# Sigmoid attention and a SiLU feed-forward on one core: four sums of x handed out one burst later in three out stages

## The chip, the core and the metric

The kernel runs on one core of a Trainium2 chip. The metric is the device time of one execution in microseconds (us), the median of several runs. PE is the engine of matmuls (PEld its loads of weights), DVE the vector engine, ACT the scalar engine with its function tables, POOL GpSimd, which issues the loads here, and SP the engine that issues the stores and the transposing DMAs. A bank is one of eight buffers in which PE leaves its results and from which DVE and ACT read them.

## The reference

```python
# q, k, v: 8 batches x 12 heads x 448 rows x 64;  w_in: 768 x 2048;  w_out: 2048 x 768
scores = q @ k.T / sqrt(64) - log(448)
attn   = sigmoid(scores) @ v                       # no softmax: no sum over a row
x      = attn.transpose(0, 2, 1, 3).reshape(3584, 768)
h      = x @ w_in
out    = (h * sigmoid(h)) @ w_out                  # float32, 3584 x 768
```

## The kernel before, in words

**Attention.** A group is four heads of one batch, so there are 24 groups, three to a batch. Each has seven rounds. A round, `scores`, is four small matmuls for scores (L223) and one sigmoid over 128 x 896 on ACT (L230). When a group's seven rounds are over, `values` multiplies by v in 28 matmuls into two banks (L254), and two scalings on DVE (L265, 128 x 448 each) move the result into xT, the transposed x of that batch in 16 bits.

**Feed-forward.** From the second pair of batches on, both products are done by a scheme of seven products in place of eight on 2 x 2 blocks (Strassen's, in Winograd's form), two batches at a time. That needs sums of the operands. `x_sums` (L355) makes four of the halves of xT for the first product: three go to tiles tx, one overwrites a half of xT. It does so in two goes: for the first two thirds of the columns' groups (four instructions over 128 x 896) once the first five of the pair's six groups have their values, and for the last third (128 x 448) behind the last group's values. `h_pair` then runs the seven products by x and w_in (L376) and SiLU.

`out_set` does the second product for two blocks of 128 rows: seven products of eight matmuls each (L502, 128 x 384 columns), with sums of the operands S made by DVE ahead (L510, L511, L514, L518) and read out by DVE. The products and what empties their banks are, in order: 1: L513; 2: L517, with the operand sum L518 behind it; 3: L523; 4: L526; 5: L529; 6: L534 and L535; 7: L539. Stores (L495) go out on SP's queue. `out_set` is a generator which gives one matmul at a time: 56 steps to a set. What an instruction on DVE stands behind is decided only by the order in which the Python code issues them; each engine takes its own in that order.

**The out stages.** For m = 0, 1 and 2 the out sets of the batches 2m and 2m + 1 (three sets for m = 0 and 2, four for m = 1) run amid the attention of the next two batches. This stage lies at some 74 to 120 us, 154 to 209 us and 242 to 289 us. Of the eight banks, six are three double buffers for scores and values, and two are left for the out matmuls; so a product waits until the one two before it has been read out. The order is a list written out by hand of pairs (rounds of scores, out matmuls behind them), such as (2, 9) or (3, 16). For each pair `burst` issues its rounds of scores and, where a group is complete, that group's `values`; it returns whether there were values. Behind it and after half of its out matmuls, `rows_if_any` is called. Behind the values of the pair's fifth group, `after_values` puts a generator with the four sums on a list, and each call of `rows_if_any` issues one of them; it also issues, where there is any, a copy with a transposing DMA for a later group. Five calls issue the four sums and take the generator off. A last burst or two follow, then what is left of the out matmuls, and the stage behind (`h_pair`), which begins with two products, the last group's values and the last third of the sums.

For m = 0 and 2 the fifth group's values stand in burst 16 of 18 (two rounds, two out matmuls), followed by (2, 9) and (3, 13). For m = 1 they stand in burst 14 of 16 (two rounds, six out matmuls), followed by (3, 16) and (2, 10).

The last out stage (m = 3) has no attention beside it and no sums of x.

Of the kernel before, what the change touches and what calls it, by code (L numbers as in the profile page):

```python
# [17 lines left out]
def kernel(  # L18
# [9 lines left out]
    nc = tc.nc  # L28
# [35 lines left out]
    def banks_for_attention(doubles):  # L64
        psum.close()
        banks.clear()
        bufs_of.update(double=doubles, single=NBANK - 2 * doubles)
        for name, bufs in bufs_of.items():
            taken[name] = 0
            new_pool(name, bufs)  # L70
# [7 lines left out]
    def banks_for_h():  # L78
        doubles = [[2 * i, 2 * i + 1] for i in longest_idle("double")]
        ring[:] = sum(doubles[:-2], [])  # L80
        ring.extend(2 * bufs_of["double"] + i for i in longest_idle("single"))
        ring.extend(sum(doubles[-2:], []))
        psum.close()
        banks.clear()
        new_pool("any", 1)
        for i in range(NBANK):
            banks[i] = banks["any"].tile([P, 512], F32, tag=f"any{i}", name=f"any{i}")
# [117 lines left out]
    def dma_transpose(g, name, copy):  # L205
        if ("k", g) not in qkT:
            new_qkT(g)
        rows = p2.tile([P, NCH, 2, D], F16, tag=f"{name}r", name=f"{name}r")
        copy(rows, flat[name, g].rearrange("p j c d -> p c j d"))
        nc.sync.dma_start_transpose(  # L210
            out=qkT[name, g], in_=rows.rearrange("p c j d -> p (c j d)")
        )
# [3 lines left out]
    def scores(g, ch):  # L216
        attnT[g, ch] = p12.tile([P, 2, S], F16, tag="attnT", name="attnT")
        psc = two_banks("psc")
        for half in range(2):
            own = slice(half * HP, (half + 1) * HP)  # L220
            for j in range(2):
                rows = slice(j * D, (j + 1) * D)
                nc.tensor.matmul(  # L223
                    psc[own, j, :S],
                    qkT["k", g][rows, ch, own],
                    qkT["q", g][rows, :, own],
                    start=True,
                    stop=True,
                )
        nc.scalar.activation(attnT[g, ch], psc[:, :, :S], AF.Sigmoid, bias=bias_s, scale=QKSCALE)  # L230
# [7 lines left out]
    def values(g, end=NCH):  # L238
        b, iq = divmod(g, NQ)
        if b not in xT:  # L240
            assert b < 2 or b - 2 in h_done
            xT[b] = p2.tile([P, NPAIR, S], F16, tag="xT", name="xT")
        pav, done_rounds = part_of.pop(g, None) or (None, 0)
        if pav is None and bufs_of["double"] > 2 and "any" not in banks:
            both = two_banks("pav")
            pav = [both[:, half] for half in range(2)]
        elif pav is None:
            pav = [one_bank("pav") for _ in range(2)]
        for ch in range(done_rounds, end):
            at = attnT.pop((g, ch))  # L250
            for half in range(2):
                own = slice(half * HP, (half + 1) * HP)
                for j in range(2):
                    nc.tensor.matmul(  # L254
                        pav[half][j * D : (j + 1) * D, :S],
                        flat["v", g][own, j, ch, :],
                        at[own, j, :],
                        start=(ch == 0),
                        stop=(ch == NCH - 1),
                    )  # L260
        if end < NCH:
            part_of[g] = pav, end
            return
        for half in range(2):
            nc.vector.tensor_scalar_mul(xT[b][:, half * NQ + iq, :], pav[half][:, :S], SX)  # L265
        if iq == NQ - 1:
            ready.add(b)
# [196 lines left out]
    def w_sums():  # L464
        for i in (2, 3, 4):
            tw[i] = cpool.tile([P, NHC, NO2], F16, tag=f"T{i}", name=f"T{i}")
        tw[1] = wq[0][1]
        for o, x, y in (
            (tw[3], wq[1][1], wq[0][1]),
            (tw[1], wq[0][1], wq[0][0]),  # L470
            (tw[2], wq[1][1], tw[1]),
            (tw[4], tw[2], wq[1][0]),
        ):
            for f in range(0, NHC, 2):
                nc.vector.tensor_sub(o[:, f : f + 2], x[:, f : f + 2], y[:, f : f + 2])
                yield
# [71 lines left out]
    sums = w_sums()  # L548
# [21 lines left out]
    def sets(m):  # L570
        for g in range(0, NCH - 1, 2):
            step = out_set(
                block(m, g), row_blocks(m, g), block(m, g + 1), row_blocks(m, g + 1)
            )
            for i, ns in enumerate(step):
                if m == 0 and g == 0 and i in (10, 14):
                    next(sums)
                if m == 0 and g == 0 and i in (20, 28, 36, 44):
                    next(in_sums)
                yield ns  # L580
        if m % 2 == 1:
            g = NCH - 1
            yield from out_set(
                kept, row_blocks(m - 1, g), block(m, g), row_blocks(m, g), m == B // 2 - 1
            )

    later, sums_of_x = [], []

    def rows_if_any(before, copy):
        if sums_of_x and next(sums_of_x[0], "end") == "end":  # L590
            sums_of_x.pop()
        if later and later[0][0] < before:
            g, name = later.pop(0)
            dma_transpose(g, name, copy)
            if name == "q":
                behind_rows(g, before)
# [3 lines left out]
    def behind_rows(g, before):  # L600
        if g + 3 >= NQB:
            return
        if g + 3 < before:
            load("kq", g + 3)
            return
        held.append(g + 3)
        if g + 1 == before:
            nc.gpsimd.tensor_copy(gate, qkT["q", g][:1, 0, :1])
            for to in held:
                load("kq", to)  # L610
            held.clear()
# [54 lines left out]
    def values_if_any():  # L666
        if waiting:
            g = waiting.pop(0)
            values(g)
            after_values(g)  # L670
            return True
        return False
# [68 lines left out]
    def burst(n, size=2):  # L741

        new = units[n : n + size]
        for u in new:
            scores(*u)
        with_values = values_if_any()
        for g, ch in new:
            if ch == NCH - 1:
                waiting.append(g)
                if 9 <= g + 3 < NQB:  # L750
                    later.extend(((g + 3, "k"), (g + 3, "q")))
        return with_values
# [16 lines left out]
    for m in range(B // 2 - 1):  # L769
        banks_for_attention(3)  # L770
        nc.scalar.activation(warm, bias_s, AF.Sigmoid)
        stream = sets(m)
        for _ in range(FIRST_DENSE):
            next(stream)
        bursts = FOUR_SETS if m % 2 else THREE_SETS
        assert sum(size for size, _ in bursts) == 2 * NT_B
        own = 2 * NQ * (m + 2)
        n = 2 * NT_B * (m + 1)
        for size, count in bursts:
            burst(n, size)  # L780
            n += size
            rows_if_any(own, nc.vector.tensor_copy)
            for i in range(count):
                next(stream)
                if i == count // 2:
                    rows_if_any(own, nc.vector.tensor_copy)
        assert not sums_of_x
        nc.scalar.activation(warm, bias_s, AF.Silu)
        for _ in stream:
            pass  # L790
        (g,) = waiting
        waiting.clear()
        banks_for_h()

        def last_values():
            values(g)
            after_values(g)
            for _ in x_sums(m + 1, NQ - 1, NQ):
                pass
            nc.gpsimd.tensor_copy(gate, tx[m + 1, 4][:1, NQ - 1, :1])  # L800

        for i, _ in enumerate(h_pair(m + 1, last_values)):
            if i % 8 == 7:
                rows_if_any(NQB, nc.gpsimd.tensor_copy)
# [33 lines left out]
```

## Time and profile before

| what | value |
|---|---|
| median of 3 runs | 365.05 us (364.96 to 365.18) |
| the profiled execution, whole | 365.46 us |
| its span, first to last instruction | 363.5 us |
| granted clock of PE | 0.997 |
| busy: PE, DVE, ACT, POOL | 98%, 69%, 69%, 21% of the span |
| one of the 12 sums over 128 x 896 (L355) | 0.61 to 0.62 us |

The page's first part gives each engine's busy time and share of the span. Matmuls are pipelined: a row of several in turn gives the start of the first and the time to the modelled end of the last. The view of waits says which engine waited for whom, in total, how often, and the longest. In the order of time each row has a start in us from the span's start, a length, an engine, a line, the written and read tiles and how many instructions are merged; brackets give the idle time before it and what ended it. Where nothing is known to have ended it, it is put under "issue".

### The profile page before, as it was taken

Reading aid. Unit: us, or ns where it says so; the run is one execution under the profiler, and the core shown is the slowest. Engines: PE = TensorE matmul, PEld = TensorE weight load, DVE = VectorE, ACT = ScalarE, POOL = GpSimd, SP = SyncE. Lnnn points to the kernel's source line nnn. Section 1 sums busy time; section 2 is a strip of 40 time slices with the busy share of each in tenths; the row PEclk is TensorE's granted clock in tenths of the full one; section 3 lists DMA queues with packets and bytes.
Section 4 is the critical chain, followed back from the end, with each engine's and each line's share of the span. In section 5 each row is a group of like instructions: output and inputs, shape, how many; then the busy total and the mean of one; then the engine's idle time right before and its main releaser. Section 6 shows DMA issues by size and latency. Waiting matters only on the chain. (4 is left out here: it accounts for less than half of the span.)

```text
span 363.5 us, 7651 instructions
## 1 busy us (share of the span) xinstructions
PE 356.1 (98%) x3036; PEld 186.8 (51%) x3036; DVE 252.2 (69%) x459; ACT 249.3 (69%) x339; POOL 77.5 (21%) x116
## 2 busy tenths in 40 slices
PE   8999999999999999999999999999999999999995
PEld 6554445555555555555555455554555555556662
DVE  3565469787666587868566768795856677797763
ACT  5999886479989756688777746679899956640000
POOL 8666511040060272000033047000100000000000
PEclk9999999999999999999999999999999999999998
DMA  8999999979969599008679569802983120003333
GB/s 138 198 204 203 204 205 203 172 114 194 163 115 207 119 133 172 0 2 160 104 133 193 105 130 165 122 2 51 166 100 88 25 65 0 3 0 88 87 88 87
DMA packets 65859, 42.80 MB, mean 118 GB/s; under 512 B 36128, under 2 KB 62496, under 8 KB 65824
## 3 DMA queue, kind: packets, MB, share of 16 engines
q0 software_dynamic: 27072, 22.58, 42.6%
q1 hardware_dynamic: 38320, 19.34, 28.0%
q8 instruction: 24, 0.39, 0.5%
q10 hardware_dynamic: 432, 0.39, 0.3%
q14 instruction: 11, 0.09, 0.1%
HBM read 45.61 MB, written 11.01 MB: 156 GB/s over the span
## 5 line engine op out<-in xcount | busy, mean ns | idle before, releaser
L230 ACT ACTIVATE attnT<-psc,bias_s 128x896 f16<-128x896 f32 x168 | 157.9, 1009 | 20.6 <-PE psc L223 19.3
L502 PEld LDWEIGHTS <-S 128*128 128x128 f16 x448 | 42.0, 98 | 33.6 <-issue 8.1
L223 PE MATMUL psc<-qT,kT 64*64 64x448 f16 x672 | 48.9, 360 | 1.1 <-ACT attnT L230 0.8
L265 DVE TENSOR_SCALAR xT<-pav 128x448 f16<-128x448 f32 x48 | 27.7, 620 | 28.9 <-PE pav L254 28.9
L502 PEld LDWEIGHTS <-gTr 128*128 128x128 f16 x336 | 31.1, 98 | 27.3 <-issue 8.7
L124 POOL DMA_DIRECT2D vf<-in_v_dram x24 | 17.3, 723 | 129.7 <-PE pav L254 122.6
L502 PE MATMUL po<-w_out_sb,gTr 128*128 128x384 f16 x224 | 41.6, 327 | 0.0
L376 PEld LDWEIGHTS <-w_in_sb 128*128 128x128 f16 x288 | 27.9, 98 | 26.7 <-issue 1.1
L502 PE MATMUL po<-T,S 128*128 128x384 f16 x224 | 41.0, 327 | 0.0
L502 PE MATMUL po<-w_out_sb,S 128*128 128x384 f16 x224 | 40.8, 326 | 0.0
L286 PE MATMUL ph<-xT,w_in_sb 128*128 128x448 f16 x192 | 38.5, 353 | 0.0
L254 PE MATMUL pav<-attnT,vf 64*64 64x448 f16 x672 | 38.1, 351 | 0.1
L376 PE MATMUL pa<-xT,w_in_sb 128*128 128x448 f16 x144 | 33.2, 353 | 0.0
L223 PEld LDWEIGHTS <-kT 64*64 64x64 f16 x672 | 17.9, 104 | 27.8 <-issue 21.3
L376 PEld LDWEIGHTS <-SI 128*128 128x128 f16 x216 | 21.1, 98 | 20.0 <-issue 0.5
L254 PEld LDWEIGHTS <-vf 64*64 64x64 f16 x672 | 21.6, 106 | 12.3 <-issue 2.9
L286 PEld LDWEIGHTS <-w_in_sb 128*128 128x128 f16 x192 | 17.8, 98 | 18.9 <-issue 3.4
L392 ACT ACTIVATE part<-pa 128x448 f32<-128x448 f32 x24 | 12.7, 543 | 18.1 <-PE pa L376 18.1
L502 PE MATMUL po<-T,gTr 128*128 128x384 f16 x112 | 21.9, 327 | 0.6 <-DVE osb L523 0.6
L370 ACT ACTIVATE gTr<-pc 128x448 f16<-128x448 f32 x24 | 13.1, 544 | 12.9 <-DVE pc L386 12.5
L386 DVE TENSOR_TENSOR part<-pb,part 128x448 f32<-128x448 f32 x24 | 14.9, 622 | 8.3 <-ACT part L392 5.0
L184 ACT ACTIVATE m<-po 128x384 f32<-128x384 f32 x1 | 0.5, 491 | 27.3 <-PE po L502 27.3
(76 smaller groups left out, 471.1 us busy)
## 6 DMA issues: line engine op xcount, KB each, us to landing
out_dram<-osb SPq DMA_DIRECT2D x52, 192.0 KB, 3.2
vf<-in_v_dram POOLq DMA_DIRECT2D x24, 224.0 KB, 6.6
kf<-in_k_dram POOLq DMA_DIRECT2D x23, 224.0 KB, 7.4
qf<-in_q_dram POOLq DMA_DIRECT2D x23, 224.0 KB, 7.8
w_in_sb<-in_moe_w_in_dram POOLq DMA_DIRECT2D x16, 192.0 KB, 7.9
w_out_sb<-in_moe_w_out_dram POOLq DMA_DIRECT2D x4, 768.0 KB, 14.9
out_dram<-osb SPq DMA_DIRECT2D x6, 96.0 KB, 2.2
kT<-kr SPq DMA_TRANSPOSE x18, 5.1
```

The source lines that it names most:

```text
L124: nc.gpsimd.dma_start(flat[name, g][:, :, c0:c1].rearrange("p i c d -> p i (c d)"), rows_in(name, g)[:, :, c0 * D : c1 * D],)
L184: nc.scalar.activation(o, i, AF.Copy)
L223: nc.tensor.matmul(psc[own, j, :S], qkT["k", g][rows, ch, own], qkT["q", g][rows, :, own], start=True, stop=True,)
L230: nc.scalar.activation(attnT[g, ch], psc[:, :, :S], AF.Sigmoid, bias=bias_s, scale=QKSCALE)
L254: nc.tensor.matmul(pav[half][j * D : (j + 1) * D, :S], flat["v", g][own, j, ch, :], at[own, j, :], start=(ch == 0), stop=(ch == NCH - 1),)
L265: nc.vector.tensor_scalar_mul(xT[b][:, half * NQ + iq, :], pav[half][:, :S], SX)
L286: nc.tensor.matmul(ph[:, :S], w_in_sb[:, cc, fc * P : (fc + 1) * P], xT[b][:, cc, :], start=(at == 0), stop=(at == NCC - 1),)
L370: nc.scalar.activation(gTr[:, r * NG + i, col + c * S : col + (c + 1) * S], h, AF.Silu, bias=0.0, scale=ISX)
L376: nc.tensor.matmul(to, w[:, n, i * P : (i + 1) * P], x[:, n], start=(start and n == 0), skip_group_check=not start, stop=(n == NQ - 1),)
L386: nc.vector.tensor_add(o, po, x)
L392: nc.scalar.activation(got[i, 1], bank[i, "a"], AF.Copy)
L502: nc.tensor.matmul(po[:, :NO2], a[:, fc, :], w[:, fc, :], start=(fc == 0), stop=(fc == NHC - 1))
```

## The change

`rows_if_any` gets a flag. With the flag off it issues no sum of x; the copies with transposing DMAs are not touched. Behind a burst with values and amid its out matmuls the flag is off. So the four sums stand behind and amid the next two bursts, which are the last two of the stage, and the generator is taken off after the loop.

```diff
-    def rows_if_any(before, copy):
-        if sums_of_x and next(sums_of_x[0], "end") == "end":
-            sums_of_x.pop()
+    def rows_if_any(before, copy, sums=True):
+        if sums and sums_of_x:
+            next(sums_of_x[0])
         if later and later[0][0] < before:
             g, name = later.pop(0)
             dma_transpose(g, name, copy)
...
         for size, count in bursts:
-            burst(n, size)
+            with_values = burst(n, size)
             n += size
-            rows_if_any(own, nc.vector.tensor_copy)
+            rows_if_any(own, nc.vector.tensor_copy, not with_values)
             for i in range(count):
                 next(stream)
                 if i == count // 2:
-                    rows_if_any(own, nc.vector.tensor_copy)
-        assert not sums_of_x
+                    rows_if_any(own, nc.vector.tensor_copy, not with_values)
+        assert next(sums_of_x.pop(), "end") == "end"
```

The order on DVE at the three places, before and after:

```
m = 0, 2  before: L265 x2, sum 1, sum 2, sum 3, L526, sum 4, L529, L534
          after:  L265 x2, sum 1, L526, sum 2, sum 3, L529, sum 4, L534
m = 1     before: L265 x2, sum 1, L517, L518, sum 2, sum 3, L523, sum 4, L526, L529, L534
          after:  L265 x2, L517, L518, sum 1, L523, sum 2, L526, sum 3, L529, sum 4, L534
```

## The prediction

> **What bounds the kernel now.** I read the page's first part, then the waits of PE, and then the order of time around the sums of x in each of the three out stages that have them.
>
> ```profile
> PE 356.1 (98%) x3036; PEld 186.8 (51%) x3036; DVE 252.2 (69%) x459; ACT 249.3 (69%) x339; POOL 77.5 (21%) x116
> ```
>
> PE is the bound from end to end. Work that moves on DVE alone, as here, is worth only the time that PE stands still for it. The waits of PE (what it waited for, us in total, times, longest) name all that the profile sees as such:
>
> ```profile
> PE pw L181 <- DVE bias_s L624: 1.1, 1, 1.1
> PE psc L223 <- ACT attnT L230: 0.8, 2, 0.5
> PE po L502 <- DVE osb L523: 0.6, 1, 0.6
> ```
>
> One row belongs to the out matmuls: one wait of 0.6 us on DVE's L523. The order of time of the second of the three stages (m = 1) shows the place; columns are start, length, engine, line, and in brackets the idle time before it.
>
> ```profile
> 200.56 1.16 DVE L265 TENSOR_SCALAR xT<-pav 128x448 f16<-128x448 f32 x2 [1.17 <-PE pav L254]
> ...
> 201.63 0.61 DVE L355 TENSOR_TENSOR tx<-xT 128x896 f16<-128x896 f16 x1
> ...
> 202.16 0.55 DVE L517 TENSOR_TENSOR osb<-po,m 128x384 f32<-128x384 f32 x1
> ...
> 202.21 2.12 PE L502 MATMUL po<-T,S 128*128 128x384 f16 x12
> 202.63 0.68 DVE L518 TENSOR_TENSOR S<-gTr,S 128x1024 f16<-128x1024 f16 x1
> 203.23 0.62 DVE L355 TENSOR_TENSOR tx<-xT,tx 128x896 f16<-128x896 f16 x1
> 203.76 0.62 DVE L355 TENSOR_TENSOR xT<-xT 128x896 f16<-128x896 f16 x1
> ...
> 204.30 0.55 DVE L523 TENSOR_TENSOR osb<-po,m 128x384 f32<-128x384 f32 x1
> 204.77 0.62 DVE L355 TENSOR_TENSOR tx<-xT,tx 128x896 f16<-128x896 f16 x1
> 204.90 0.81 PE L502 MATMUL po<-T,gTr 128*128 128x384 f16 x4 [0.57 <-DVE osb L523]
> ```
>
> DVE works without a gap from 200.56 on and is late: three sums stand ahead of L523, which empties the bank that product 5 needs (two banks alternate, so product k needs product k-2 read out). L523 ends at 204.30 + 0.55 = 204.85, and PE starts at 204.90.
>
> How long PE really stood still comes from starts. A lone out matmul's row is 0.34 us long and the mean of the out groups is 0.327, but 12 in a row take 2.12, so they start every (2.12 - 0.327)/11 = 0.163 us. The last of the 12 started at 202.21 + 2.12 - 0.327 = 204.00, and the next was due at 204.17. The loss is 204.90 - 204.17 = **0.73 us**, 0.16 more than the bracket, which counts from the modelled end of the matmul before. So a stall of up to 0.16 us is in no row of waits. The first stage (m = 0) has just such a one:
>
> ```profile
> 115.68 0.62 DVE L355 TENSOR_TENSOR tx<-xT 128x896 f16<-128x896 f16 x1
> ...
> 117.41 0.55 DVE L526 TENSOR_TENSOR osb<-po,osb 128x384 f32<-128x384 f32 x1
> ...
> 117.69 0.34 PE L502 MATMUL po<-T,gTr 128*128 128x384 f16 x1
> ...
> 118.01 2.27 PE L502 MATMUL po<-w_out_sb,S 128*128 128x384 f16 x13
> ```
>
> The step from product 5 to product 6 takes 118.01 - 117.69 = 0.32 instead of 0.163, and L526, which frees product 6's bank, ends at 117.96: a loss of **0.16 us**. The third stage (m = 2) repeats it: L526 ends at 286.54, and PE goes from 286.27 to 286.59, 0.16 again:
>
> ```profile
> 285.99 0.55 DVE L526 TENSOR_TENSOR osb<-po,osb 128x384 f32<-128x384 f32 x1
> ...
> 286.27 0.34 PE L502 MATMUL po<-T,gTr 128*128 128x384 f16 x1
> ...
> 286.59 2.76 PE L502 MATMUL po<-w_out_sb,S 128*128 128x384 f16 x16
> ```
>
> A page of the Trainium skill, Perfetto Trace Analysis (section Identifying the Most-Contended Engine), says that matmul busy time misjudges PE because pipelined matmuls look smaller in a trace than they are. The sum by the busy rows would be 0.57 us, by starts 1.05; the trace agrees with the page in that two of three stalls have no row.
>
> **The change, part by part.** Nothing is added or removed: four tensor_subs in each of three stages go to a later place in DVE's queue. PE, ACT, POOL and SP keep their instructions in the same order, no DMA moves past another, and none of the four sums issues one. They are needed only in the stage behind, after the last values and the last third of the same sums (L376 reads tx from 125.6 us on in the first of the three); that order stays. One sum costs DVE 0.53 us from start to start (203.23 to 203.76), L517 or L523 0.47 (202.16 to 202.63), L518 0.60 (202.63 to 203.23).
>
> Stage m = 1, new order L265 x2, L517, L518, sum 1, L523, sum 2, L526, sum 3, L529, sum 4, L534. L517 takes the first sum's place at 201.63 (product 2's last matmul belongs to a pair started at 200.44, over by 201.0). L518 starts at 202.10, sum 1 at 202.70, L523 at 203.23; product 3's last matmul, fourth of the 12, ends at 202.21 + 3 x 0.163 + 0.33 = 203.03, so PE isn't late for it. L523 ends at 203.78, and product 5 can start at its due 204.17, with 0.35 to spare: 0.73 us saved. What is late next? Sum 2 runs from 203.70, and L526 waits for product 4 (over at 204.33): 204.40 to 204.95. Sum 3 follows. L529 waits for product 5, as today, 0.73 earlier (207.01 to 206.28), and sum 4 fits into the 0.74 us that DVE idles ahead of L534 today. L526 also waits for the store of the tile it overwrites: those two stores were issued at 197.03 and 197.54 and landed 5.4 to 6.8 us later, by 204.34 at worst, and PE needs L526's bank only for product 6, which starts at 206.81 today and so at 206.08. That covers it.
>
> Stage m = 0, new order sum 1, L526, sum 2, sum 3, L529, sum 4, L534. Sum 1 stays at 115.68; L526 moves from 117.41 to 116.21 and ends at 116.76, 1.1 us before product 6 is due at 117.69 + 0.163 = 117.85. Sums 2 and 3 run from 116.68 to 117.84. L529 waits for product 5's last matmul (over at 118.03) and ends at 118.60; product 7 needs that bank at 117.85 + 8 x 0.163 = 119.16, so 0.56 to spare. Sum 4 ends its turn at 119.05, L534 is due at 119.35. Saved: 0.16. Stage m = 2 is the same, 168.58 us later: 0.16.
>
> Does it last? ACT's sigmoids of the last burst are not moved in m = 0 and m = 2, since they come before the stall; in m = 2 its table load and the two copies of L392 that follow end at 291.27 as today. PE needs the first of them only when it adds to that bank, about 292.4. The sums that the stage behind reads, and POOL's gate, all follow PE. So I count the whole of it.
>
> Sum: 0.73 + 0.16 + 0.16 = 1.05 us. Against the profiled execution (365.46 us; span 363.5 and 1.96 around it) that gives 364.4. It stood 0.41 above the median of 365.05, so a median of **364.0 us**. A difference of 0.2% (0.73 us, below 364.32) is about what a measurement here can tell from none.
>
> **Rivals.**
> - Only a part: the two 0.16 us steps aren't DVE's doing (the trace puts them under "issue"), or only part of them goes. For it: no row names L526 as releaser. Against it: PE starts 0.05 us after L526's end in both, as after L523's in m = 1. Then 0.57 to 0.73 is left, 364.3 to 364.5. Chance 0.10.
> - Given back: PE, earlier, meets a wait that was hidden, such as a store that lands over 1.1 us later than the worst here ahead of L526 in m = 1 (DMA is busy 62% of 198 to 211 us, and fuller before that), or ACT at the start of the next stage. PE's waits show no such candidate after the three places. 365.0. Chance 0.08.
> - The change does nothing: excluded as far as the order goes, since L523 and L526 do stand ahead of sums that were ahead of them; counted with the case above.
> - Slower: the stall moves one product on. In m = 0 and m = 2, sums 1 to 3 now stand between the scaling and L529, and product 7 waits for L529. If each sum took e longer in its new place, L529 would end at 118.30 + 3e, and PE would lose 3e - 0.86 in each of the two; in m = 1, L523 costs e - 0.35. At e = 0.72, the length of POOL's load issue that could stand in DVE's way, this is 1.30 + 1.30 + 0.37 = 2.97, so 365.05 - 1.05 + 2.97 = 367.0; it is slower from e of about 0.45 on. Against it: all twelve sums take 0.61 to 0.62 today, and POOL's one issue near them ends before each new place (115.60 against 115.68; 201.53 against 202.70). Chance 0.04. The Trainium skill's SBUF — State Buffer (section SBUF: two separate sides) has a rule for such a mechanism: a DVE instruction with two SBUF inputs, as these sums are, and a GpSimd instruction that reads SBUF block each other for a whole instruction. By it e would rise only where POOL reads SBUF beside the sums, and the trace shows no POOL copy there.
>
> **How the numbers follow.** Forecast 0.78, wholly below 364.32; the partial case 0.10, divided about evenly by the bound; given back 0.08, same; slower 0.04, most of it by over 0.2%. Faster 0.82, same 0.15, slower 0.03. The forecast's own bounds come from the spread of the three runs (0.2) and 0.05 per reading of a start: 363.8 to 364.25. The range goes on to 364.5 for the partial case.
>
> **What would show it.** In the changed trace: no bracket of DVE L523 on PE in m = 1, and product 4 to product 5 in one 0.163 step; 0.16 instead of 0.32 between products 5 and 6 in m = 0 and m = 2; L526 right behind sum 1 there; sum 4 ahead of L534, with L534 still waiting for PE. I am wrong if PE's starts show a new gap ahead of product 6 or 7, if sums take over 0.62, or if the stage behind starts no earlier.

## The result, and the profile after

The changed kernel takes 364.07 us (median of 8 runs, 363.60 to 364.35) against 365.05 us before (364.92 to 365.46). The ratio is 0.9969, with a 95% interval from 0.9959 to 0.9980: 1.1 us less by the ratio (0.7 to 1.5), 0.98 by the medians. The prediction was 364.0 us.

The profiled execution takes 364.17 us, its span 362.2. First the waits of PE in the changed kernel, in full:

```profile
PE pw L181 <- DVE bias_s L624: 1.1, 1, 1.1
PE psc L223 <- ACT attnT L230: 0.8, 2, 0.5
PE psc L223 <- DVE qT L201: 0.3, 1, 0.3
```

The row for L523 is gone; the rest is as it was. Now the order of time in the second stage (m = 1) of the changed kernel:

```profile
201.16 0.55 DVE L517 TENSOR_TENSOR osb<-po,m 128x384 f32<-128x384 f32 x1
...
201.63 0.68 DVE L518 TENSOR_TENSOR S<-gTr,S 128x1024 f16<-128x1024 f16 x1
201.74 2.12 PE L502 MATMUL po<-T,S 128*128 128x384 f16 x12
202.22 0.62 DVE L355 TENSOR_TENSOR tx<-xT 128x896 f16<-128x896 f16 x1
202.76 0.55 DVE L523 TENSOR_TENSOR osb<-po,m 128x384 f32<-128x384 f32 x1
...
203.70 0.81 PE L502 MATMUL po<-T,gTr 128*128 128x384 f16 x4
203.90 0.56 DVE L526 TENSOR_TENSOR osb<-po,osb 128x384 f32<-128x384 f32 x1
...
206.28 0.62 DVE L355 TENSOR_TENSOR tx<-xT,tx 128x896 f16<-128x896 f16 x1
...
207.11 0.56 DVE L534 TENSOR_TENSOR osb<-po,osb 128x384 f32<-128x384 f32 x1 [0.21 <-PE po L502]
```

L523 now ends at 203.31, before product 5's turn, and the row of product 5 has no bracket. The last of the 12 matmuls starts at 201.74 + 2.12 - 0.327 = 203.53, and product 5 follows at 203.70. Sum 4 stands ahead of L534, which still waits for PE (0.21 us), so the sum costs nothing there.

The first stage (m = 0) of the changed kernel:

```profile
115.36 0.61 DVE L355 TENSOR_TENSOR tx<-xT 128x896 f16<-128x896 f16 x1
...
115.89 0.55 DVE L526 TENSOR_TENSOR osb<-po,osb 128x384 f32<-128x384 f32 x1
...
117.37 0.34 PE L502 MATMUL po<-T,gTr 128*128 128x384 f16 x1
117.54 2.76 PE L502 MATMUL po<-w_out_sb,S 128*128 128x384 f16 x16
117.74 0.56 DVE L529 TENSOR_TENSOR osb<-osb,po 128x384 f32<-128x384 f32 x1 [0.23 <-PE po L502]
```

and the third (m = 2):

```profile
285.07 0.34 PE L502 MATMUL po<-T,gTr 128*128 128x384 f16 x1
285.25 2.76 PE L502 MATMUL po<-w_out_sb,S 128*128 128x384 f16 x16
```

The step from product 5 to product 6 is 0.17 to 0.18 us in both, where it was 0.32. Now 16 matmuls run in one row over the border of products 6 and 7, with no gap.

The spans differ by 1.3 us, more than the three stalls. I set every start of a matmul in one trace against the same start in the other. Apart from the three places, no step behind the first 6.5 us differs by over 0.02 us, but the first 6.5 us are 0.33 us shorter: the transposes of the first k begin at 5.28 us before and at 4.88 us after. The two rows, before and after:

```profile
5.28 0.32 PE L194 MATMUL ptrk<-ident,kf 128*64 128x128 f16 x2
```

```profile
4.88 0.32 PE L194 MATMUL ptrk<-ident,kf 128*64 128x128 f16 x2
```

Nothing is changed there. The profiled executions below differ from each other likewise, up to 28 us in, two executions of the changed kernel among them: it is spread between executions.

### The profile page after: what moved, and what is told of

The parts are those of the page before. It is cut to its first block, busy times and chain, and to the rows that moved or that the text cites. A ratio compares the mean times of both kernels' runs of the same rounds, so it can differ in the third digit from the quotient of the medians.

```text
span 362.2 us, 7652 instructions
## 1 busy us (share of the span) xinstructions
PE 355.6 (98%) x3036; PEld 186.9 (52%) x3036; DVE 252.2 (70%) x459; ACT 249.2 (69%) x339; POOL 77.5 (21%) x116
## 4 chain that ended last, share of the span: by engine, by line
PE 96%; ACT 1%; DVE 1%; issue 0%; ACTq 0%
PE po L502 37%; PE psc L223 11%; PE ph L286 9%; PE pav L254 9%; PE pa L376 8%; PE pd L376 8%; PE pc L376 8%; PE pb L376 4%; PE pw L181 2%; ACT attnT L230 1%; PE ptrq L194 1%; PE ptrk L194 1%; DVE kT L201 0%; DVE qT L201 0%; ACT tx L300 0%
## 5 line engine op out<-in xcount | busy, mean ns | idle before, releaser
L502 PEld LDWEIGHTS <-S 128*128 128x128 f16 x448 | 42.0, 98 | 33.3 <-issue 7.7
L502 PEld LDWEIGHTS <-gTr 128*128 128x128 f16 x336 | 31.1, 98 | 26.5 <-issue 7.9
L502 PE MATMUL po<-w_out_sb,gTr 128*128 128x384 f16 x224 | 41.6, 327 | 0.0
L502 PE MATMUL po<-T,S 128*128 128x384 f16 x224 | 41.0, 327 | 0.0
L502 PE MATMUL po<-w_out_sb,S 128*128 128x384 f16 x224 | 40.8, 327 | 0.0
L502 PE MATMUL po<-T,gTr 128*128 128x384 f16 x112 | 21.9, 327 | 0.0
```

What stands on the lines that cost most here:

```text
L502: nc.tensor.matmul(po[:, :NO2], a[:, fc, :], w[:, fc, :], start=(fc == 0), stop=(fc == NHC - 1))
```

## The experiments

The measure that tells most is a single step of PE, from one matmul's start to the next, at the place where it is longer than its usual 162 to 172 ns. From the traces, in ns (p4 is the step into product 4, and so on; the last column is what the three stages lose over the changed kernel). The ratios below are to the kernel before, run beside each set: its median was 365.14 us beside the first four kernels below and 365.24 beside the last four.

| kernel | m = 0 | m = 1 | m = 2 | lost, us |
|---|---|---|---|---|
| before | p6 321 | p5 892 | p6 322 | 1.03 |
| changed | p6 172 | p5 163 | p6 172 | 0 |
| changed, again | same | same | same | 0 |
| m = 1 only | p6 318 | p5 163 | p6 321 | 0.30 |
| m = 0 and 2 only | p6 172 | p5 891 | p6 172 | 0.73 |
| all early | p6 857 | p4 1785 | p6 858 | 2.99 |
| all late | p7 299 | p7 491 | p7 302 | 0.61 |
| doubled | p7 667, values + 267 | p5 485 | p7 664, values + 260 | 1.86 |
| late and doubled | p7 2282 | p7 2472 | p7 2280 | 6.55 |
| on POOL | p6 172 | p5 527 | p6 172 | 0.36 |

**The changed kernel again** (no edit).

> The changed kernel once more, beside the others. Theory: PE loses nothing at the three places, so about 1.05 us below the kernel before, 364.0. Rival (part of the first measurement was spread at the head of the kernel, where the changed kernel's profile was 0.32 us shorter with nothing changed there): the start-to-start loss at the three places is gone all the same, while the head's length comes and goes between executions of one kernel.

363.95 us, ratio 0.9967 (0.9954 to 0.9979). The three steps are short again. In the head, its starts run 0.2 us ahead of the first execution of the same kernel at 14 us, 0.4 behind it at 15 us and 0.33 behind from 25 us on. So the gain is at the three places, and the spread is in the head.

**The change in one stage alone.** The diff is against the changed kernel; the call amid the out matmuls gets the same flag, and `next` a default, since a fifth call can find the generator at its end.

```diff
-            next(sums_of_x[0])
+            next(sums_of_x[0], None)
...
-            rows_if_any(own, nc.vector.tensor_copy, not with_values)
+            rows_if_any(own, nc.vector.tensor_copy, not (with_values and m == 1))
```

> The change in the second out stage (m = 1) alone. Theory (three stalls of PE behind DVE, priced by matmul starts): the 0.73 us of m = 1 go, the two steps of 0.32 us from product 5 to 6 in m = 0 and m = 2 stay: 365.05 - 0.73 = 364.3. Rival (the bracket of the profile is the price): 365.05 - 0.57 = 364.5. Rival (the gain comes from elsewhere, so the place doesn't matter): 364.0 or 365.05.

364.55 us, ratio 0.9980 (0.9972 to 0.9989), that is 0.73 us less than before (0.4 to 1.0). The time alone can't tell the price by starts, 0.73, from the rival's price by the bracket, 0.57: both lie in that interval, and the median of 364.55 is nearer the rival's 364.5. The step into product 5 of m = 1 can: it goes from 892 to 163 ns, 0.73 us. The steps in m = 0 and m = 2 stay long, here in m = 0 of this kernel:

```profile
117.58 0.34 PE L502 MATMUL po<-T,gTr 128*128 128x384 f16 x1
...
117.89 0.97 PE L502 MATMUL po<-w_out_sb,S 128*128 128x384 f16 x5
```

0.31 us and no bracket: a stall that only the starts show. The other part, with `m != 1` in the same place:

> The change in the first and third out stages alone. Theory: two steps of 0.32 us become 0.17, the wait of 0.57 us on L523 in m = 1 stays: 365.05 - 0.31 = 364.7. Rival (the 0.16 us steps are an issue gap and not DVE's): the steps stay at 0.32 and the time at 365.05.

364.91 us, ratio 0.9994 (0.9985 to 1.0003); 0.2 us less, which the time alone can't tell from nothing. The trace can: both steps are 172 ns, and m = 1 keeps its wait:

```profile
204.30 0.81 PE L502 MATMUL po<-T,gTr 128*128 128x384 f16 x4 [0.56 <-DVE osb L523]
```

So the 0.15 us steps were DVE's, not an issue gap, and the parts add up: 0.73 + 0.30 = 1.03, all that the whole change removes.

**All four sums right behind the burst with values.** The opposite of the change: `rows_if_any` issues all that is left, whatever the burst (the call amid the out matmuls likewise).

```diff
-            next(sums_of_x[0])
+            list(sums_of_x[0])
...
-            rows_if_any(own, nc.vector.tensor_copy, not with_values)
+            rows_if_any(own, nc.vector.tensor_copy)
```

> All four sums in one go right behind the burst with values, in each stage. Theory: in m = 0 and m = 2 L526 stands behind four sums and ends 0.53 us later than today, so product 6 is late by 0.57 us each; in m = 1 L517 stands behind four sums and ends about 1.48 us after product 4 is due, and L523 then costs nothing more. Sum 1.48 + 2 x 0.57 = 2.6 us over the changed kernel: 366.6 to 366.7, slower than both. Rival (DVE, at 70%, has room, so the order of the sums moves nothing beyond what was seen): no more than 365.05.

367.19 us, ratio 1.0052 (1.0040 to 1.0065). The mechanism holds, the loss is 2.99 us instead of 2.62. The order of time in m = 1 of this kernel:

```profile
202.00 0.62 DVE L355 TENSOR_TENSOR tx<-xT 128x896 f16<-128x896 f16 x1
...
202.66 0.62 DVE L355 TENSOR_TENSOR tx<-xT,tx 128x896 f16<-128x896 f16 x1
203.20 0.62 DVE L355 TENSOR_TENSOR xT<-xT 128x896 f16<-128x896 f16 x1
203.73 0.62 DVE L355 TENSOR_TENSOR tx<-xT,tx 128x896 f16<-128x896 f16 x1
204.27 0.55 DVE L517 TENSOR_TENSOR osb<-po,m 128x384 f32<-128x384 f32 x1
...
204.87 1.46 PE L502 MATMUL po<-T,S 128*128 128x384 f16 x8 [1.46 <-DVE osb L517]
```

L517 stands behind four sums, and product 4 behind L517. From sum 2 to 3, and 3 to 4, it is 0.54, as reckoned; from sum 1 to sum 2 it is 0.66. Sum 2 reads what sum 1 writes. That is 0.12 of the 0.14 us by which m = 1 exceeds its 1.48. In m = 0 and m = 2 the long step stood in the kernel before already (115.68 to 116.33), so it explains nothing there; the expectation's own terms, 0.16 lost today and L526 0.53 later, add up to 0.69 and not to its 0.57, and 0.685 was measured.

**All four behind the last burst** (`at == len(bursts) - 1` as the flag, and the same `list`).

> All four sums in one go behind the last burst of the stage. Theory: DVE waits ahead of L529 anyway, so the four fit: in m = 0 and m = 2 L529 ends at the moment product 7 is due (a loss of 0 to 0.05 us), in m = 1 0.15 us behind it. Sum 0.1 to 0.3 us: 364.1 to 364.4. Rival (the sums are now too late for the stage behind, or their place counts and not their cover): over 364.7.

364.70 us, ratio 0.9982 (0.9973 to 0.9991): between the two kernels, about 0.5 us over the changed one, and over the expected 364.1 to 364.4. The rival by which the sums come too late for the stage behind falls all the same: behind the head, only the three steps into product 7 are longer. In m = 0:

```profile
115.77 0.61 DVE L355 TENSOR_TENSOR tx<-xT 128x896 f16<-128x896 f16 x1
116.42 0.62 DVE L355 TENSOR_TENSOR tx<-xT,tx 128x896 f16<-128x896 f16 x1
...
117.02 0.34 PE L502 MATMUL po<-T,gTr 128*128 128x384 f16 x1
117.20 2.90 PE L502 MATMUL po<-w_out_sb,S 128*128 128x384 f16 x16
117.50 0.62 DVE L355 TENSOR_TENSOR tx<-xT,tx 128x896 f16<-128x896 f16 x1
118.03 0.55 DVE L529 TENSOR_TENSOR osb<-osb,po 128x384 f32<-128x384 f32 x1
```

DVE is again without a gap up to L529, and L529 ends at 118.58 where product 7 is due at 117.20 + 8 x 0.163 = 118.50. PE starts another 0.05 us behind L529's end. The stall is hidden in the 2.90 of 16 matmuls, where 2.76 is usual. The expected 0.1 to 0.3 us became 0.61, in the main by the 0.65 from sum 1 to sum 2 (0.12 three times) and by PE's 0.05 (three times).

**The sums doubled**, first in the changed kernel's places.

```diff
-            nc.vector.tensor_sub(o[:, of], x[:, of], y[:, of])
+            [nc.vector.tensor_sub(o[:, of], x[:, of], y[:, of]) for _ in range(2 if lo == 0 and o is not y else 1)]
```

> The changed kernel with sums 1, 2 and 4 issued twice (the same values again), in their new places; this prices the rival of the prediction by which the stall moves one product on. Theory, from the changed kernel's own starts: in m = 0 and m = 2 L529 ends 0.22 us after product 7 is due, in m = 1 L523 ends 0.17 us after product 5 is due, and sum 4 twice costs PE nothing. Sum 0.6 us over the changed kernel: 364.7. Rival (DVE's spare time takes it): 364.07, no step of PE longer.

366.06 us, ratio 1.0022 (1.0010 to 1.0035): slower than before. The place was right, the size wrong, 1.86 us instead of 0.6. The order of time in m = 0 of this kernel:

```profile
118.46 1.27 DVE L355 TENSOR_TENSOR tx<-xT,tx 128x896 f16<-128x896 f16 x2
...
119.65 0.62 DVE L355 TENSOR_TENSOR xT<-xT 128x896 f16<-128x896 f16 x1
120.18 0.55 DVE L529 TENSOR_TENSOR osb<-osb,po 128x384 f32<-128x384 f32 x1
120.65 1.28 DVE L355 TENSOR_TENSOR tx<-xT,tx 128x896 f16<-128x896 f16 x2
120.78 1.46 PE L502 MATMUL po<-w_out_sb,S 128*128 128x384 f16 x8 [0.34 <-DVE osb L529]
...
122.97 0.56 DVE L539 TENSOR_TENSOR osb<-po,osb 128x384 f32<-128x384 f32 x1
...
123.31 1.78 PE L254 MATMUL pav<-attnT,vf 64*64 64x448 f16 x28
```

A pair on the same tile costs 0.65 + 0.54 from start to start (118.46 to 119.65), not twice 0.53: 0.24 us more ahead of L529 and 0.12 ahead of L523. And PE starts 0.05 us behind the end of the instruction it waits for (L529 ends at 120.73), which the expectation had left out. With both, its 0.22 and 0.17 become 0.51 and 0.34; 0.50 and 0.32 were measured. And sum 4 twice isn't free: it holds up L534 to L539, L539 ends at 123.53, and the last values behind take over its bank: their second matmul waits for it, 0.27 us. This stall too is hidden in a length (1.78 where 1.52 is usual).

**Late and doubled**, both edits.

> All four sums behind the last burst, and sums 1, 2 and 4 issued twice there: seven instructions in a row ahead of L529. Theory: three more of 0.53 us use up the cover, product 7 is late by about 1.6 us in m = 0 and m = 2 and 1.7 us in m = 1: 4.9 us over the changed kernel, 369.0. Rival (L529 isn't what holds product 7): under 365.

370.94 us, ratio 1.0163 (1.0134 to 1.0192). L529 does hold product 7: the profile has "PE po L502 <- DVE osb L529" three times, 6.1 us in total, and the steps lose 6.55 us. That is 1.65 over the expected sum, of which four dependent steps in each stage, 0.12 longer than reckoned, explain 1.4, and PE's 0.05 behind L529's end another 0.15.

**The sums on POOL**, `(nc.gpsimd if lo == 0 else nc.vector).tensor_sub(...)`.

> The changed kernel with the four sums on POOL instead of DVE. Theory: no stall of PE behind DVE is left, so freeing DVE of 2.1 us in each stage gives nothing: 364.0, as the changed kernel. Rival: POOL takes about two times the 0.92 us of its copies of this size for each sum, so the last ends some 7.5 us later; if the stage behind then waits for it, or DVE's instructions with two operands in SBUF are held up by POOL's reads beside them (as the Trainium skill's SBUF - State Buffer, section SBUF: two separate sides, says for such pairs), 364.5 or more.

364.51 us, ratio 0.9980 (0.9968 to 0.9992), about 0.4 us over the changed kernel: the rival's time, not the theory's 364.0. In m = 0 and m = 2 no step is longer, as the theory said, and the stage behind waits for no sum of POOL's. In m = 1 one step is longer, by the rival's second way:

```profile
201.37 1.90 POOL L355 TENSOR_TENSOR tx<-xT 128x896 f16<-128x896 f16 x1
...
201.90 1.92 DVE L518 TENSOR_TENSOR S<-gTr,S 128x1024 f16<-128x1024 f16 x1
...
203.75 0.55 DVE L523 TENSOR_TENSOR osb<-po,m 128x384 f32<-128x384 f32 x1
204.34 0.81 PE L502 MATMUL po<-T,gTr 128*128 128x384 f16 x4 [0.20 <-DVE osb L523]
```

L518, which has both operands in SBUF, takes 1.92 us beside POOL's sum instead of 0.68, and ends 0.55 us behind the sum's end at 203.27. It was held until POOL was done; L523 behind it comes too late for product 5. L517 and L523, which read one operand from a bank, keep their 0.55. This is the blocking that the Trainium skill's SBUF — State Buffer (section SBUF: two separate sides) states, and the trace agrees.

## Why the prediction was right

**The mechanism** (PE stands still only where a sum stands ahead of the instruction that frees its bank): shown by both partial kernels, by the order turned the other way, and by what doubling does.

**The size.** Predicted 0.73 + 0.16 + 0.16 = 1.05 us; the steps lost 0.729, 0.149 and 0.150, in all 1.03 (the usual step into product 6 is 0.172, not 0.163). The steps show this size; the time's interval, 0.7 to 1.5, would not, and that the median came within 0.1 us of the forecast is in part luck, as the eight executions spread from 363.60 to 364.35. Reading starts rather than brackets made the difference: the brackets sum to 0.57, and the first and third stages would have been called nothing. The reading that matmul busy time misleads, with which the prediction cited the Trainium skill's Perfetto Trace Analysis, holds: PE is 98% busy in both profiles. Its reason is another here: the rows do not look too small, they last 327 ns at a step of 163, and so overlap and cover a short stall.

**The new order in time.** Every start that was worked out can be compared once the 0.32 us by which the changed kernel's starts lie ahead there is added (and 0.15 more in m = 1, for what m = 0 saved). L526 in m = 0: 116.21 predicted, 115.89 + 0.32 found. L529: 118.05 and 117.74 + 0.32. L523 in m = 1: 203.23 and 202.76 + 0.47. L529 there: 206.28 and 205.81 + 0.47.

**What is late next.** Nothing, as predicted: the covers for product 5 (m = 1) and product 7 (m = 0 and 2) held. The first is 0.35 us as predicted. The second is 0.5 and not 0.56: the prediction counted PE's 0.05 us behind the end of L523 in the one, and not behind the end of L529 in the other. They are real and small. Doubling used them up.

**The rivals.** Partial gain: fell, both short stalls went. Given back: fell, every step behind the places is as before. Slower: its premise, sums that take longer in their new place, did not come; they take 0.61 to 0.62. Its arithmetic is tested by the doubled kernel: sums 1 and 2 twice put 2 x 0.65 = 1.3 us more ahead of L529, in the place of 3e, and 1.3 - 0.86 = 0.44, where 0.505 was measured (0.49 with the missing 0.05); in m = 1 sum 1 twice puts 0.65 ahead of L523, and 0.65 - 0.35 = 0.30, where 0.322 was.

**Not seen:** that a sum behind the one whose result it reads takes 0.65 and not 0.53. The profile before had it, with sum 1 at 115.68 and sum 2 at 116.33. It did not matter for the forecast, since in the new order no sum stands right behind one that it reads, but it was missing in four of the later expectations, in the first of them for m = 1 alone.

## What to carry to other kernels

Where PE is the bound, an instruction on an engine with time to spare costs what it delays: list what frees PE's banks, note when each bank is due, and put work that nobody waits for behind the one that somebody does. Measure PE's stalls from start to start; here a stall under 0.16 us, the 327 ns of a row less the step of 163, shows in no bracket, only in a step or a row a little too long. Then reckon how much more each place would bear: here it was 0.35 and 0.5 us, and the doubled sums, which took more, turned a gain of 1.0 us into a loss.

## What the runs showed of the hardware

Two instructions in turn on DVE, over 128 x 896 in 16 bits, are 0.53 to 0.54 us apart from start to start when the second does not touch what the first writes (203.20 to 203.73 in m = 1 of the kernel with all sums early), and 0.65 to 0.66 when it does (202.00 to 202.66 there).

POOL's tensor_sub over 128 x 896 took 1.87 to 1.90 us against DVE's 0.62, and 2.22 where it started beside the held L518.

In the late and doubled kernel PE lost 2.3 us behind product 6 in m = 1, and then ran at half its clock for a while. Busy time in two stretches around it (us, then busy us and instructions of PE, PEld, DVE, ACT, POOL, then the granted clock, the share of DMA, and GB/s):

```profile
208.00:211.50 3.50, 1.42 (x9) 0.74 (x8) 3.40 (x6) 2.67 (x4) 0.00 (x0) 1.00 0.00 0
211.50:214.80 3.30, 3.24 (x10) 1.43 (x10) 1.51 (x4) 0.00 (x0) 0.00 (x0) 0.50 0.45 115
```

The matmuls start every 320 ns there instead of 163, which cost this execution 1.6 us more. In m = 0 and m = 2, where PE lost 2.1 us, it did not happen. The Trainium skill's TensorE: Matmul & The Clock Gate (section Part 1: The HAM clock gate) says that the clock is halved after at least one idle window of about 3.4 us, and that the window runs freely; here less than that sufficed, once in three. The length of the stall need not be what decided: the trace's record of the clock has the half clock from 211.52 to 214.94 us, that is 3.41 us, and full clock for the 204.80 us before, 60 times 3.413. On that grid, PE was idle for 2.11 us of the step before the drop (208.11 to 211.52), and for at most 1.82 and 1.51 us of any step around the other two stalls, which lie elsewhere on the grid; so length and place can't be told apart here. Four of this kernel's six executions took 370.7 to 371.0 us at a mean granted clock of 0.997 to 0.999. The profiled one took 372.47 us at 0.993, and the sixth 373.98 at 0.989.
